# Kernel block 0 of a convolution and feed-forward kernel: bank tiles, buffer order, norm shifts on GpSimd, a split doubling

## The chip, the cores and the metric

The kernel runs on one core of one Trainium2 chip. The metric is the device time of one execution in microseconds. Before the change the median of 3 runs is 1348.77 us (1348.36 to 1349.15).

## The reference

One sequence of 2048 tokens with 576 channels goes through two residual branches, each behind a layer norm whose scale and shift come from a conditioning vector: a long convolution per channel, and a feed-forward layer with 4608 hidden units.

```python
mod = (_silu(c) @ w_mod).reshape(c.shape[0], 6, 1, -1)
sa, ca, ga, sb, cb, gb = (mod[:, 0], ..., mod[:, 5])
h = _layernorm(x) * (1 + ca) + sa
x = x + ga * conv(h)
h = _layernorm(x) * (1 + cb) + sb
x = x + gb * (relu(h @ w1) @ w2)

# conv(u), for L = 2048 and 128 states per channel
dt = exp(log_dt); A = -exp(log_A_real) + 1j * A_imag
C = (C_real + 1j * C_imag) * dt[:, None]
K = 2 * einsum("dn,dnl->dl", C, exp((A * dt[:, None])[:, :, None] * arange(L))).real
y = irfft(rfft(u, 2 * L) * rfft(K, 2 * L), 2 * L)[:, :L] + u * D_skip
```

## The kernel before

The 2048 tokens are four blocks of 512. The feed-forward layer of each block is a long series of matmuls (L1326 and L1351) that starts after the convolution of block 0 and then keeps TensorE occupied to the end. The convolutions of blocks 1 to 3 run as Python generators beside it: `step` in `ffn` takes pieces of them between matmuls, four times for every two series of 14 matmuls, and a piece that yields -1 ends that step. Block 0's convolution, and the kernel K for it, have nothing to hide behind; they fill the first 215 us or so.

The convolution kernel K comes from class `KGen`. The 576 channels are 6 groups of 96 (two halves of 48, index u). An exponent l in the range 0 to 511 is written as 16 times 32, so that K's values for a group are a product of two factor tables: W1 (16 powers, times C) and W2 (32 powers). `first` does this for the groups in three chunks of two groups:

- `raw(c)` makes the phases of a chunk (`turns`: ACT scales `th` and rounds it to an integer `k`, DVE subtracts at L133, 22 times) and the magnitudes (`exps`, on ACT). In chunk 1 it also normalizes the input `h` of block 0: `center` on ACT, for all four slices of `h`, and `affine` on GpSimd, for slices 0 and 1.
- `values(g)` turns them into W2, in two calls of `half_values` (odd, then even): sines on ACT into PSUM tiles `s`, cosines on ACT into SBUF tiles `c` (three buffers), products on DVE (L172, L173) and on GpSimd (the helper `pool` at L59, tiles `W<-c,E`). `start` (L179, L201) writes the first entry of W1, `powers` the factors `Zp` and `zs`. A function `then` is called between the two halves.
- `double(g)` fills W1 by doubling in four steps (`doubling`: DVE at L246, L247, L249, L250, for groups 4 and 5 through the helper at L510; the adds of the last step on GpSimd, tiles `W<-T,T`).
- `multiply(g)` multiplies W1 and W2 on TensorE (L262, 384 small matmuls for a group, "product g" in what follows) into one half of the PSUM tile `kps`, and `rows(g)` copies that out on ACT (tile `ke`). For every three groups the result is stored (`kd`, on SP's queue) and loaded again in another layout (`kt`, L1259).

For g in (0, 2) the order of the calls is: raw(g/2 + 1); double, (at g = 0: affine of slices 2 and 3), multiply, for groups g and g + 1; values(g + 2); values(g + 3) with rows(g) between its halves; rows(g + 1). After that come, from `conv0`: the transform of the input (L758, tile `ZU`), double(4), multiply(4) with the transform of K (`ZK`) in between, double(5), multiply(5). ZU takes SBUF space of the factor tiles, the tables of the transform (`early`, two DMAs from `fcu` and `fck` on SP's queue) one of the three buffers of W1.

What orders the work: each engine runs its instructions in a fixed order that the framework's scheduler has settled when the program is built, by the order of the calls and by when it expects inputs to be there. Instructions marked `keep_in_program_order` (on ACT and GpSimd nearly all of these; from `conv0` on also those through `kept`) keep the order of the calls. Waits go by tile: an instruction that reads or writes a tile waits for the earlier instructions on that tile that it conflicts with, and a new tile in a rotating buffer waits until every user of the old one is done.

In blocks 1 to 3, `inverse` does the transform back in four steps (two matmuls at L1019 into one PSUM buffer, then an add on DVE into `x2`), and `conv` runs it for p = 0 beside `spec_K(1)`.

Of the kernel before, what the change touches and what calls it, by code (L numbers as in the profile page):

```python
# [18 lines left out]
P = 128  # L19
# [6 lines left out]
G = 96  # L26
# [20 lines left out]
class KGen:  # L47
# [13 lines left out]
    def open(self, early, late):  # L61
# [6 lines left out]
        self.ph = pool(late, "kg_ph", "right", space=PSUM)  # L68
        self.kps, self.banks = self.ph.tile([P, 2, 512], F32, name="kps"), 0
        self.factors = ExitStack()  # L70
# [4 lines left out]
    def bank(self):  # L75
        self.banks += 1
        return self.kps[:, self.banks % 2]

# [37 lines left out]
    def turns(self, w):  # L116
# [3 lines left out]
        th = self.th[:, w].rearrange(pair, u=2)  # L120
        if w.start:
            t = self.kps[:, :, 384 : 384 + G]
            self.act(t, th, AF.Copy)
            th = t
        for slots in TURNS:
# [22 lines left out]
    def half_values(self, g, W2, E, f, odd):  # L148
# [31 lines left out]
        for u in range(2):  # L180
            uc = slice(u * H, u * H + H)
            p(W2[u][:, 0, hi], c[:, :, uc], Eh[:, :, uc], op=ALU.mult)
            p(W2[u][:, 0, lo][:, ::-1], c[:, 0:n, uc], El[:, 0:n, uc][:, ::-1], op=ALU.mult)
            if not odd:
                nc.gpsimd.tensor_copy(W2[u][:, 0, 23], El[:, 7, uc])
                nc.gpsimd.memset(W2[u][:, 1, 23], 0.0)

    def start(self, g, s15, c15):

        v = self.nc.vector.tensor_tensor  # L190
        W1 = self.W1[g] = self.pc.tile([P, 2, 16, 2, H], F32, tag="W1", bufs=3, name=f"W1_{g}")
        gs = slice(g * G, (g + 1) * G)
# [31 lines left out]

    def doubling(self, g):

        v, p = self.k.v if g > NG - 3 else self.nc.vector.tensor_tensor, self.pool
        W1, Z = self.W1[g], self.Z[g][0]
        flat = "p u a r c -> p u (a r) c"
        for i, m in enumerate((1, 2, 4, 8)):  # L230
            X, out = W1[:, :, 0:m].rearrange(flat), W1[:, :, m : 2 * m]
# [39 lines left out]
    def first(self, setup, mod, norm):  # L271
# [5 lines left out]
        def raw(c):  # L277
# [4 lines left out]
            if c == 1:  # L282
                for i in range(4):
                    center(i)
                for i in range(2):
                    affine(i)
# [29 lines left out]

        def double(g):
            self.doubling(g)
            for u in range(2):
# [18 lines left out]

        load, stats, scale, center, affine = norm
        next(mod)  # L340
# [8 lines left out]
        for g in (0, 2):  # L349
            raw(g // 2 + 1)  # L350
            for i in (g, g + 1):
                double(i)
                if g == 0:
                    affine(i + 2)
                multiply(i)
            values(g + 2, lambda: None)
            if g == 2:
                t = k.early = self.pc.tile([P, 2, 4, 2, P], F32, tag="W1", bufs=3, name="early")
                for i, n in enumerate(("fcu", "fck")):
                    nc.sync.dma_start(out=t[:, i], in_=k.I[n])  # L360
            values(g + 3, lambda: rows(g))
            rows(g + 1)
        yield
        double(4)
        between = yield
# [122 lines left out]
class Body:  # L488
# [164 lines left out]
    def norm0(self, kg):  # L653
# [15 lines left out]

        def center(i):  # L670
            kg.act(h[:, i], h[:, i], AF.Identity, scale=rs[i][:, 3:4], bias=rs[i][:, 4:5])

        def affine(i):
            kg.pool(h[:, i], h[:, i], self.m["ca"], op=ALU.mult)
            kg.pool(h[:, i], h[:, i], self.m["sa"], op=ALU.add)
# [3 lines left out]

        return load, stats, scale, center, affine  # L680

# [188 lines left out]
    def conv(self, s):  # L870
# [76 lines left out]
        def inverse(p, V):  # L947
            ops = lambda n2: [(self.gc[:, n2, c, :], V[:, n2, c]) for c in range(2)]
            return self.inverse(x2, p, ops)

# [60 lines left out]

    def inverse(self, x2, p, ops, order=(0, 2, 1, 3)):

        xv = x2.rearrange("m n (dd p q) -> m n dd p q", dd=4, p=2)
        for n2 in order:
# [8 lines left out]
            self.v(xv[:, n2, :, p], pv, xv[:, n2, :, p], op=ALU.add)  # L1024
            yield 0.45

    def norm2(self, s, x2, xp, st=None):
# [554 lines left out]
```

## Time and profile before

| | us |
|---|---|
| median of 3 runs | 1348.77 |
| the profiled execution | 1344.2 |
| its span, first to last instruction | 1342.4 |
| TensorE busy in the span | 1220.4 (91%) |
| DVE busy | 870.2 (65%) |
| ACT busy | 503.6 (38%) |
| GpSimd busy | 195.1 (15%) |
| mean granted TensorE clock | 0.946 |

Times in the profile count from the span's first instruction. PE is TensorE, PEld its weight loads, DVE is VectorE, ACT is ScalarE, POOL is GpSimd, SP the engine whose queue issues most DMAs. "L133" is line 133 of the kernel. A row of the timeline has start, length, engine, line, operation, output and inputs, shapes and a count; the brackets give idle time before it and what ended it. Neighbouring instructions of one kind are merged into one row, and instructions of one engine overlap a little, so that the length of one is somewhat more than the distance to the next.

### The profile page before, as it was taken

What the parts mean: (1) busy time and instruction counts of PE and PEld (TensorE: products, weight loads), DVE (VectorE), ACT (ScalarE), POOL (GpSimd) and SP (SyncE); (2) the same over time, 40 slices, a digit from 0 to 9 for tenths busy, and PEclk for the clock granted to TensorE, in tenths of its full rate; (3) what the DMA queues carried; (4) which work ended last, traced back from release to release, by engine and by line L of the source; (5) the groups of instructions that cost most, each with busy time, mean ns of one, the idle gap of its engine ahead of it and who ended that gap; (6) DMA issues with size and microseconds to landing.
All of it is one profiled execution on the core that took longest, in us unless ns stands there. A gap on an engine that the chain in (4) does not pass through costs nothing.

```text
span 1342.4 us, 26042 instructions
## 1 busy us (share of the span) xinstructions
PE 1220.4 (91%) x10608; PEld 974.6 (73%) x10608; DVE 870.2 (65%) x1351; ACT 503.6 (38%) x1014; POOL 195.1 (15%) x271
## 2 busy tenths in 40 slices
PE   5124798999999998999999899999999999999998
PEld 3124566788787786787777787787888888888886
DVE  5978997999887899389546886276988222111111
ACT  7986234222224322622243225343322353232331
POOL 1777231111120100111101000100010000000000
PEclk9555898899999998999999999999999999999999
DMA  6676399888798875698779894757997556666651
GB/s 198 239 256 230 133 365 373 330 290 299 272 362 284 307 277 183 215 396 324 242 262 320 284 356 149 260 183 278 318 347 232 170 181 212 197 197 201 194 169 62
DMA packets 132424, 340.47 MB, mean 254 GB/s; under 512 B 22352, under 2 KB 22672, under 8 KB 132304
## 3 DMA queue, kind: packets, MB, share of 16 engines
q1 hardware_dynamic: 105200, 215.21, 48.3%
q0 software_dynamic: 26816, 123.01, 25.0%
q8 instruction: 83, 1.36, 0.4%
q10 hardware_dynamic: 288, 0.59, 0.1%
q14 instruction: 37, 0.30, 0.1%
HBM read 258.55 MB, written 80.22 MB: 252 GB/s over the span
## 4 chain that ended last, share of the span: by engine, by line
PE 74%; DVE 10%; DMA 7%; issue 5%; ACT 2%; POOL 1%; SPq 0%; DVEq 0%; ACTq 0%; POOLq 0%
PE hps L1326 30%; PE acc L1351 29%; PE kps L440 5%; PE ps_f L758 3%; PE kps L262 3%; DMA Ua<-Ud 3%; DVE T L510 2%; PE ps_i L1019 2%; DMA Ud<-U 1%; DVE k L133 1%; DVE Y L510 1%; DMA W1d<-W 1%; PE kps L607 1%; ACT c L56 1%; DVE W L510 1%
## 5 line engine op out<-in xcount | busy, mean ns | idle before, releaser
L1351 PE MATMUL acc<-hh,w 128*128 128x512 f32 x1296 | 420.5, 400 | 2.1 <-DVE w L510 2.0
L1326 PE MATMUL hps<-xh,w 128*128 128x512 f32 x1152 | 396.2, 404 | 1.9 <-ACT xh L1082 1.9
L1351 PEld LDWEIGHTS acc<-hh,w 128*128 128x128 f32 x1296 | 243.9, 189 | 55.1 <-DVE w L510 2.8
L1332 DVE SCALAR_TENSOR_TENSOR hl<-hps,hh 128x512 fp32r<-128x512 f32 x144 | 99.2, 689 | 279.1 <-ACT hh L1331 278.9
L1351 PE MATMUL acc<-hl,w 128*128 128x512 f32 x720 | 279.9, 399 | 0.0
L1326 PEld LDWEIGHTS hps<-xh,w 128*128 128x128 f32 x1152 | 218.2, 190 | 50.1 <-ACT xh L1082 3.5
L1326 PE MATMUL hps<-xl,w 128*128 128x512 f32 x576 | 231.3, 402 | 0.2 <-DVE xl L1087 0.2
L1331 ACT ACTIVATE hh<-hps 128x512 fp32r<-128x512 f32 x144 | 86.1, 598 | 341.7 <-PE hps L1326 329.5
L1304 ACT ACTIVATE w<-r 128x576 fp32r<-128x576 f32 x144 | 98.7, 686 | 237.5 <-issue 182.8
L1351 PEld LDWEIGHTS acc<-hl,w 128*128 128x128 f32 x720 | 135.8, 189 | 28.1
L1326 PEld LDWEIGHTS hps<-xl,w 128*128 128x128 f32 x576 | 109.5, 190 | 24.9 <-DVE xl L1087 1.5
L262 PE MATMUL kps<-W,W 128*32 128x16 f32 x2304 | 40.3, 217 | 73.4 <-POOL W L59 49.5
L1297 ACT ACTIVATE w<-r 128x640 fp32r<-128x640 f32 x142 | 104.0, 732 | 3.0 <-DMA r<-in_w_dram 3.0
L1326 PE MATMUL hps<-xs,w 128*128 128x512 f32 x288 | 97.4, 418 | 3.5 <-DVE hl L1332 3.4
L262 PEld LDWEIGHTS kps<-W,W 128*32 128x32 f32 x2304 | 37.9, 150 | 77.6 <-POOL W L59 50.9
L510 DVE TENSOR_TENSOR Y<-Y,T 128x1152 f32<-128x1152 f32 x64 | 84.9, 1353 | 0.1
L440 PEld LDWEIGHTS kps<-W1r,W2r 128*32 128x32 f32 x3456 | 63.7, 146 | 23.2 <-issue 17.7
L440 PE MATMUL kps<-W1r,W2r 128*32 128x48 f32 (+2 forms) x3456 | 71.1, 237 | 4.4 <-issue 4.3
L759 ACT ACTIVATE Z<-ps_f 128x288 f32<-128x288 f32 x104 | 42.3, 407 | 64.9 <-PE ps_f L758 62.5
L1326 PEld LDWEIGHTS hps<-xs,w 128*128 128x128 f32 x288 | 53.2, 190 | 16.5 <-DVE hl L1332 4.8
L510 DVE TENSOR_TENSOR W<-Z 128x576 f32<-128x576 f32 x52 | 37.0, 755 | 39.9 <-ACT Z L759 39.7
L510 DVE TENSOR_TENSOR w<-r,w 128x512 fp32r<-128x512 f32 (+2 forms) x108 | 58.2, 578 | 2.9 <-ACT w L1304 2.9
(216 smaller groups left out, 1366.7 us busy)
## 6 DMA issues: line engine op xcount, KB each, us to landing
r<-in_w_dram SPq DMA_DIRECT2D x144, 320.0 KB, 4.0
r<-in_w_dram SPq DMA_DIRECT2D x144, 288.0 KB, 3.6
w<-L1d SPq DMA_DIRECT2D x108, 320.0 KB, 3.0
w<-L2d SPq DMA_DIRECT2D x108, 288.0 KB, 3.1
W2r<-W2d POOLq DMA_DIRECT2D x18, 1536.0 KB, 9.2
W2d<-W SPq DMA_DIRECT2D x10, 1536.0 KB, 7.4
W<-W1d POOLq DMA_DIRECT2D x18, 768.0 KB, 9.2
Ua<-Ud POOLq DMA_DIRECT2D x12, 1152.0 KB, 9.9
```

What stands on the lines that cost most here:

```text
L262: self.nc.tensor.matmul(ps[32 * dd : 32 * dd + 32, 12 * u + q, :], W2[:, r, :, ch], W1[:, u, :, r, ch], start=(r == 0), stop=(r == 1),)
L440: nc.tensor.matmul(ps[32 * dd : 32 * dd + 32, q, :], W2[:, r, :, ch], W1[:, :na, r, ch], start=(r == 1), stop=(r == 0),)
L510: return self.kept(self.nc.vector.tensor_tensor(*args, **kw))
L758: kept(nc.tensor.matmul(o, fc[:, n2, c, :], src(n2), start=True, stop=True))
L759: nc.scalar.activation(Z[:, n2, c], ps[:, :PC], AF.Copy)
L1019: self.nc.tensor.matmul(ps[:, :PC], a, b, start=(i == 0), stop=(i == len(todo) - 1))
L1297: nc.scalar.activation(w[:, 0], r, AF.Copy)
L1304: nc.scalar.activation(w[:, 0:D], r2[g], AF.Copy)
L1326: nc.tensor.matmul(ps, a, x, start=(i == 0), stop=(i == 13))
L1331: nc.scalar.activation(hh, ps, AF.Relu)
L1332: nc.vector.scalar_tensor_tensor(hl, ps, 0.0, hh, op0=ALU.max, op1=ALU.subtract)
L1351: nc.tensor.matmul(acc[i], a, x, start=(f == 0 and j in (0, 3, 6, 9, 12)), stop=(f == NF - 1 and j in (2, 5, 8, 11, 13)),)
```

## The change

- The PSUM tile `kps` with two banks becomes two tiles of one bank each. The copy of `th` into that tile, made for chunks 1 and 2, is dropped with it: L133 then reads `th` from SBUF.
- `center` goes. `affine(i)` subtracts the mean and multiplies by the reciprocal root in one tensor_scalar on GpSimd ahead of its two other instructions. For slices 0 and 1 it stays in raw(1); for slices 2 and 3 it moves from between the doublings to the end of the round g = 0, behind rows(1).
- Doubling takes a list of steps. Steps 0 and 1 of groups 2 and 4 run inside values(g + 3), behind rows(g); steps 2 and 3 where the whole doubling was.
- `place(5)` allocates W1 of group 5 ahead of the tables.
- The copy at L185 is kept in program order.
- In blocks 2 and 3, for p = 0, `inverse` yields -1 after each of its four adds.

```diff
--- before.py
+++ after.py
@@ -66,7 +66,7 @@
         self.pa, self.ss = pool(early, "kg_a", "left"), pool(early, "kg_s", "left", space=PSUM)
         self.pw, self.pc = (pool(late, f"kg_{x}", "right") for x in "wc")
         self.ph = pool(late, "kg_ph", "right", space=PSUM)
-        self.kps, self.banks = self.ph.tile([P, 2, 512], F32, name="kps"), 0
+        self.kps, self.banks = [self.ph.tile([P, 512], F32, name=f"kps{i}") for i in range(2)], 0
         self.factors = ExitStack()
         self.pt = pool(self.factors, "kg_t", "right")
         self.ps = pool(self.factors, "kg_ps", "right", space=PSUM)
@@ -74,7 +74,7 @@
 
     def bank(self):
         self.banks += 1
-        return self.kps[:, self.banks % 2]
+        return self.kps[self.banks % 2]
 
     def setup(self, I):
         nc, pc = self.nc, self.pc
@@ -118,10 +118,6 @@
         F = []
         pair = "p (u c) -> p u c"
         th = self.th[:, w].rearrange(pair, u=2)
-        if w.start:
-            t = self.kps[:, :, 384 : 384 + G]
-            self.act(t, th, AF.Copy)
-            th = t
         for slots in TURNS:
             n = len(slots)
             k = self.pa.tile(
@@ -182,13 +178,18 @@
             p(W2[u][:, 0, hi], c[:, :, uc], Eh[:, :, uc], op=ALU.mult)
             p(W2[u][:, 0, lo][:, ::-1], c[:, 0:n, uc], El[:, 0:n, uc][:, ::-1], op=ALU.mult)
             if not odd:
-                nc.gpsimd.tensor_copy(W2[u][:, 0, 23], El[:, 7, uc])
+                self.tc.keep_in_program_order(nc.gpsimd.tensor_copy(W2[u][:, 0, 23], El[:, 7, uc]))
                 nc.gpsimd.memset(W2[u][:, 1, 23], 0.0)
 
+    def place(self, g):
+        if g not in self.W1:
+            self.W1[g] = self.pc.tile([P, 2, 16, 2, H], F32, tag="W1", bufs=3, name=f"W1_{g}")
+        return self.W1[g]
+
     def start(self, g, s15, c15):
 
         v = self.nc.vector.tensor_tensor
-        W1 = self.W1[g] = self.pc.tile([P, 2, 16, 2, H], F32, tag="W1", bufs=3, name=f"W1_{g}")
+        W1 = self.place(g)
         gs = slice(g * G, (g + 1) * G)
         T = self.ps.tile([P, 512], F32, tag="T", name="Tc")[:, : 2 * G]
         T = T.rearrange("p (x u c) -> p x u c", x=2, u=2)
@@ -222,12 +223,13 @@
             p(zs[:, :, r], zs[:, :, r], e[:, 4:6], op=ALU.mult)
         self.Z[g] = Z, zs
 
-    def doubling(self, g):
+    def doubling(self, g, steps):
 
         v, p = self.k.v if g > NG - 3 else self.nc.vector.tensor_tensor, self.pool
         W1, Z = self.W1[g], self.Z[g][0]
         flat = "p u a r c -> p u (a r) c"
-        for i, m in enumerate((1, 2, 4, 8)):
+        for i in steps:
+            m = 1 << i
             X, out = W1[:, :, 0:m].rearrange(flat), W1[:, :, m : 2 * m]
             zr, zi = (
                 Z[:, r, i].rearrange("p (u c) -> p u c", u=2).unsqueeze(2).broadcast_to([P, 2, 2 * m, H])
@@ -280,8 +282,6 @@
                 scale()
             F = self.turns(w)
             if c == 1:
-                for i in range(4):
-                    center(i)
                 for i in range(2):
                     affine(i)
             E = dict((m, self.exps(w, m)) for m in (2, 3, 0, 1, 4))
@@ -314,8 +314,10 @@
             for u in range(2):
                 save(k.Zd[2 * g + u], zs[:, :, :, u * H : u * H + H], g == NG - 1)
 
-        def double(g):
-            self.doubling(g)
+        def double(g, steps=range(4)):
+            self.doubling(g, steps)
+            if steps[-1] < 3:
+                return
             for u in range(2):
                 save(
                     strips(k.W1d[2 * g + u], 2),
@@ -336,7 +338,7 @@
             if g % 3 == 2:
                 self.store(0, g // 3, ke[0].rearrange("p a q -> p (a q)"), nc.sync)
 
-        load, stats, scale, center, affine = norm
+        load, stats, scale, affine = norm
         next(mod)
         load()
         raw(0)
@@ -349,19 +351,21 @@
         for g in (0, 2):
             raw(g // 2 + 1)
             for i in (g, g + 1):
-                double(i)
-                if g == 0:
-                    affine(i + 2)
+                double(i, range(2, 4) if i == 2 else range(4))
                 multiply(i)
             values(g + 2, lambda: None)
             if g == 2:
+                self.place(5)
                 t = k.early = self.pc.tile([P, 2, 4, 2, P], F32, tag="W1", bufs=3, name="early")
                 for i, n in enumerate(("fcu", "fck")):
                     nc.sync.dma_start(out=t[:, i], in_=k.I[n])
-            values(g + 3, lambda: rows(g))
+            values(g + 3, lambda: (rows(g), double(g + 2, range(2))))
             rows(g + 1)
+            if g == 0:
+                for i in (2, 3):
+                    affine(i)
         yield
-        double(4)
+        double(4, range(2, 4))
         between = yield
         multiply(4, between)
         yield
@@ -667,17 +671,17 @@
         def scale():
             rs.extend(self.norms(st, True))
 
-        def center(i):
-            kg.act(h[:, i], h[:, i], AF.Identity, scale=rs[i][:, 3:4], bias=rs[i][:, 4:5])
-
         def affine(i):
+            self.tc.keep_in_program_order(self.nc.gpsimd.tensor_scalar(
+                h[:, i], h[:, i], rs[i][:, 0:1], rs[i][:, 3:4], op0=ALU.subtract, op1=ALU.mult
+            ))
             kg.pool(h[:, i], h[:, i], self.m["ca"], op=ALU.mult)
             kg.pool(h[:, i], h[:, i], self.m["sa"], op=ALU.add)
 
         def load():
             self.nc.sync.dma_start(out=h, in_=self.I["x"][0].rearrange("n m d -> m n d"))
 
-        return load, stats, scale, center, affine
+        return load, stats, scale, affine
 
     def pool(self, ctx, name, **kw):
         return ctx.enter_context(
@@ -946,7 +950,7 @@
 
         def inverse(p, V):
             ops = lambda n2: [(self.gc[:, n2, c, :], V[:, n2, c]) for c in range(2)]
-            return self.inverse(x2, p, ops)
+            return self.inverse(x2, p, ops, spaced=s > 1 and p == 0)
 
         def back(p, Y):
             V = self.spec(f"V_{s}_{p}")
@@ -1009,7 +1013,7 @@
             v(y, y, T, op=op or ALU.add)
             yield 1.35
 
-    def inverse(self, x2, p, ops, order=(0, 2, 1, 3)):
+    def inverse(self, x2, p, ops, order=(0, 2, 1, 3), spaced=False):
 
         xv = x2.rearrange("m n (dd p q) -> m n dd p q", dd=4, p=2)
         for n2 in order:
@@ -1023,6 +1027,8 @@
             pv = ps[:, :PC].rearrange("m (dd q) -> m dd q", dd=4)
             self.v(xv[:, n2, :, p], pv, xv[:, n2, :, p], op=ALU.add)
             yield 0.45
+            if spaced:
+                yield -1
 
     def norm2(self, s, x2, xp, st=None):
 
```

## The prediction

> **What bounds the kernel now.** I read the clock first, then busy time by stretches, then the chain of waits and the list of who waits for whom over the first 200 us.
>
> ```profile
> 76.00:90.00 14.00, 4.19 (x248) 3.87 (x241) 7.63 (x20) 9.61 (x22) 14.00 (x21) 0.50 0.56 211
> 90.00:104.00 14.00, 0.00 (x0) 0.00 (x0) 13.83 (x41) 13.97 (x52) 4.68 (x8) 0.50 0.78 271
> 118.00:132.00 14.00, 6.50 (x254) 4.92 (x246) 7.77 (x20) 9.70 (x20) 14.00 (x22) 0.50 0.85 303
> 300.00:1342.00 1042.00, 1025.52 (x6911) 822.95 (x6909) 613.12 (x851) 346.45 (x619) 77.20 (x110) 0.99 0.74 250
> ```
>
> Columns: stretch, length, busy time of PE, weight load, DVE, ACT, GpSimd, granted clock, DMA share, GB/s. From 300 us on TensorE is busy 1025.5 of 1042 us: what is won ahead of it shifts everything behind it. Ahead of it the bound changes hands: GpSimd is busy 14.0 of 14.0 in 76 to 90 and in 118 to 132 (half_values), DVE and ACT in 90 to 104 (turns, exps, doubling), while TensorE waits.
>
> ```profile
> 81.85 1.70 PE kps L262 x88
> 83.58 0.49 ACT ke L56
> 84.06 0.73 ACT c L56
> 89.66 5.91 DVE k L133 x22
> ```
> ```profile
> ACT ke L56 <- PE kps L262: 18.6, 3, 13.5
> DVE W L179 <- PE kps L262: 2.7, 1, 2.7
> ACT c L56 <- POOL W L59: 2.5, 1, 2.5
> 79.72 3.75 POOL L59 TENSOR_TENSOR W<-c,E 128x384 f32<-128x384 f32 x4
> ```
>
> The chain goes from product 1 into ACT's copy `ke` of product 0 at 83.58: a wait by tile, since product 0 is the first half of those matmuls. Then come group 3's even half, and the turns of groups 4 and 5 (L133) at 89.66.
>
> **The change part by part.**
>
> *Two bank tiles.* The `ke` copies of rows(0) and rows(2) stop waiting for the next product. Alone this is worth almost nothing: ACT's next `c` needs a buffer that GpSimd reads until 79.72 + 3.75 = 83.47, the same moment as 83.58. What makes it pay is that GpSimd gets there earlier.
>
> *Norm on GpSimd.*
>
> ```profile
> 51.97 3.13 ACT L56 ACTIVATE h<-h,mv 128x576 f32<-128x576 f32 x4
> L59 POOL TENSOR_TENSOR h<-h,m_sa 128x576 f32<-128x576 f32 x4 | 5.7, 1435 | 0.2
> L59 POOL TENSOR_TENSOR h<-h,m_ca 128x576 f32<-128x576 f32 x4 | 5.7, 1414 | 4.5 <-ACT h L56 4.5
> L59 POOL TENSOR_TENSOR zs<-zs,E 128x192 f32<-128x192 f32 x12 | 6.9, 604 | 0.0
> L185 POOL COPY W<-E 128x48 f32<-128x48 f32 x12 | 2.7, 228 | 30.5 <-ACT E L56 30.5
> ```
>
> ACT loses four instructions, 3.13 us, ahead of exps; DVE is still doubling when exps end, so I cost that at nothing. The tensor_scalar (one tensor input, 576 columns) isn't in the trace: not under the 0.60 of an op a third as wide, not over the 1.43 of two inputs; I take 0.8, nearer the low end, since a one-input COPY of 48 columns costs 0.23 in all. affine for two slices is then 2 x (0.8 + 1.41 + 1.44) = 7.3 us. affine(0) and (1) start 4.5 us sooner than now. affine(3), 2.85 us, leaves the stretch that GpSimd bounds: `c` no longer waits 2.5, and the turns at 89.66 come about 2.8 earlier. But affine(2) and (3) now stand behind half_values(3) in GpSimd's queue, ahead of the adds of double(2), and those feed TensorE.
>
> *The PSUM copy of th goes.* The title doesn't say so, but L133 now reads `th` and `k` both from SBUF, while GpSimd has work. The one place that shows such a meeting:
>
> ```profile
> 174.84 2.75 DVE L510 TENSOR_TENSOR W<-Z 128x576 f32<-128x576 f32 x4
> 177.63 3.37 DVE L510 TENSOR_TENSOR U<-W 128x576 f32<-128x576 f32 x6
> 176.15 2.10 POOL L1130 TENSOR_TENSOR kt<-kt,fcU 1x288 f32<-1x288 f32 x1 [11.04 <-DMA kt<-kd]
> 155.53 2.90 DVE L510 TENSOR_TENSOR U<-W 128x576 f32<-128x576 f32 x6
> ```
>
> By the widths above the GpSimd op should take 0.8; it took 2.10, ending at 178.25, just past the end of the four back-to-back DVE ops (177.59). DVE lost about 0.5 afterwards (3.37 for six ops that take 2.90 undisturbed at 155.53). So a running stream of DVE ops with two SBUF inputs shuts GpSimd out, and one GpSimd op in flight delays DVE once. L133 is such a stream, 22 ops in 5.91. In turns of chunk 1 the 4.5 us idle above covers most of it. In chunk 2 nothing does: GpSimd loses 5.9, DVE about 0.5 (bounds: 0 and 5.9 for GpSimd).
>
> *Split doubling.* Steps 0 and 1 of group 2 move ahead of the turns, into DVE's waits for ACT:
>
> ```profile
> 95.48 0.35 DVE L247 TENSOR_TENSOR T<-W,Zp 128x192 f32<-128x192 f32 x1
> 96.32 0.55 DVE L246 TENSOR_TENSOR t<-W,Zp 128x384 f32<-128x384 f32 x1
> 98.04 0.55 DVE L246 TENSOR_TENSOR t<-W,Zp 128x384 f32<-128x384 f32 x1
> 68.71 3.94 POOL L59 TENSOR_TENSOR W<-T,T 128x384 f32<-128x384 f32 x4 [0.99 <-DVE T L247]
> 92.27 1.17 POOL L59 TENSOR_TENSOR zs<-zs,E 128x192 f32<-128x192 f32 x2
> 102.98 3.93 POOL L59 TENSOR_TENSOR W<-T,T 128x384 f32<-128x384 f32 x4 [0.34 <-DVE T L247]
> ```
>
> From 95.48 to 98.04, 2.6 us leave the path; the same again for group 4. DVE would be ready for the adds of 102.98 at 102.98 - 2.8 - 2.6 + 0.5, about 98. GpSimd isn't: now it works without a real pause from 68.71 to 93.44, that is 24.7 us; less 2.85, plus 7.3, plus 5.9 makes 35.1, so the adds start at about 104, not 98. **GpSimd takes DVE's place**, and product 2 starts 1 us later than now. Double(3) and the halves behind it still gain: their GpSimd work runs on without a pause, about 4 us earlier than now.
>
> *Group 5's tile ahead of the tables.* W1_5 takes the buffer that product 2 frees, so DVE's 2.7 us wait goes. The tables take the one that product 3 frees.
>
> ```profile
> 104.03 0.30 PE L262 MATMUL kps<-W,W 128*32 128x16 f32 x2 [20.50 <-POOL W L59]
> 124.22 1.72 PE L262 MATMUL kps<-W,W 128*32 128x16 f32 x99 [1.56 <-issue]
> 116.78 0.37 SPq L360 DMA_DIRECT2D early<-in_fcu_dram  x1
> early<-in_fcu_dram SPq DMA_DIRECT2D x1, 512.0 KB, 6.2
> 133.11 0.71 ACT L759 ACTIVATE ZU<-ps_f 128x288 f32<-128x288 f32 x2 [2.16 <-POOL W L59]
> 140.77 0.28 PE L262 MATMUL kps<-W,W 128*32 128x16 f32 x2 [2.05 <-POOL W L59]
> 166.27 6.55 PE L758 MATMUL ps_f<-h,early 128*128 128x288 f32 x16
> ```
>
> Products 2 and 3 take 104.03 to 125.94, 21.9 us, with waits between instruction blocks rather than on data. One later start: 127; table issued, 6.2 to landing: 133.2; the 16 matmuls of ZU, 6.55: product 4 at 139.8, 1.0 ahead of 140.77. The stores of `kd` stand behind the tables on SP's queue, and DVE waits for the reload of `kt` between doubling 4 and 5, so DVE's large lead (2.6 + 4 + 2.7) also shrinks, to about 3. I take 2 for the whole stage, between 1 and 3; the DMA-bound stretch after it starts that much earlier with the same work.
>
> *A yield after each inverse step of blocks 2 and 3.*
>
> ```profile
> 764.26 0.40 PE L1351 MATMUL acc<-hl,w 128*128 128x512 f32 x1
> 768.72 2.29 PE L1019 MATMUL ps_i<-V,gc 128*128 128x288 f32 x4 [4.06 <-DVE x L510]
> 790.00:800.00 10.00, 10.00 (x46) 8.27 (x45) 10.00 (x9) 3.14 (x5) 0.00 (x0) 1.00 1.04 391
> 800.00:810.00 10.00, 10.00 (x46) 8.29 (x45) 10.00 (x10) 2.60 (x4) 0.00 (x0) 1.00 0.72 219
> ```
>
> TensorE idles 4.06 us before block 2's second inverse step, for DVE. The yield puts that step one stop later, seven matmuls of 10.00 / 46 = 0.22 us, 1.6 us of other work in the gap. I take 1.6 won. Bounds: the whole 4.06 and, below nothing, 3 lost: three stops with little in them, and DVE already full at 790 to 810 ahead of block 2's end.
>
> Sum: -2 - 1.6 = -3.6 against the profiled execution, 1344.2 us (span 1342.4): 1340.6. The runs' median, 1348.77, lies 4.6 above it: **1345.2**.
>
> **The rivals.**
>
> 1. *GpSimd is not shut out.* Drop the 5.9: adds at 98, product 3 done at 121, table there by 127; GpSimd's last `c` reads, which hold up ZU now until 133.11, end about 6 earlier; kt comes early too. Stage gain 6, with the yield 7.6: 1341. For it: one meeting in the trace is thin evidence, and L133 ops, 0.27 apart, wait for ACT one by one and may leave gaps.
>
> 2. *GpSimd and DVE take turns op by op* (slower). Each L133 then waits for one GpSimd op while GpSimd has any queued. In chunk 1 nine are queued: the last `c` product, two zs and six of affine, some 1.0 + 1.2 + 7.3 = 9.5 us, so L133 ends about 9 later, and again in chunk 2; the gains above (2.8, twice 2.6, 2.7) give back some 10 of 18: +8, 1356. It decides when more than about four GpSimd ops get in per chunk. Against it: the op at 176.15 let DVE's later, independent ops pass. [...]
>
> 3. *The queue behind GpSimd and the yields cost more.* With tensor_scalar at 1.43, four times 0.63 more, product 3 ends 2.5 later, so product 4 starts 1.5 later than now, and the yields lose 3: +4.5, 1353.
>
> That the copies wait for the bank and not the tile, so that splitting does nothing, is excluded by `ke` at 83.58.
>
> **How the numbers follow.** Forecast 0.49, its own range 1342.5 to 1348.5; rival 1 0.27; rival 2 0.12; rival 3 0.12. A measurement here can tell about 0.2%, 2.7 us, from no change. Faster: rival 1 and six tenths of the forecast, 0.56. Same: the rest of the forecast and half of rival 3, 0.26. Slower: 0.18. The range 1339.5 to 1351.5 takes in the bounds of the port and of the yields and leaves out rival 2 and the far ends of 1 and 3.
>
> **What would show it.** In the changed profile: `ke` of rows(0) well before product 1 ends; the turns of chunk 2 starting near 86.5; GpSimd with a hole of some 6 us during them and the adds of double(2) near 104; the table's issue just after product 3, near 127; product 4 near 140; the idle before the second inverse step of block 2 at 2.5 us. I am wrong if GpSimd runs through the turns (rival 1), if L133 spreads over far more than 6 us (rival 2), or if product 4 starts after 141 (rival 3).

## The result, and the profile after

The changed kernel takes 1358.18 us (median of 6 runs, 1354.83 to 1359.42) against 1348.57 for the kernel before on the same chip (6 runs, 1343.22 to 1349.15). The ratio is 1.0071, with a 95% interval of 1.0052 to 1.0089: **slower by 0.7%**, where 1345.2 was forecast and 1351.5 was the upper end of the range. The profiled execution of the changed kernel took 1354.83 us (span 1353.0).

First the groups of instructions by line of the kernel before, from 40 to 125 us (busy time in us and mean of one in ns behind the first bar):

```profile
L133 DVE SCALAR_TENSOR_TENSOR k<-kps,k 128x192 f32<-128x192 f32 x44 | 11.9, 351 | 0.0
```

The same view and stretch of the kernel after:

```profile
L129 DVE SCALAR_TENSOR_TENSOR k<-th,k 128x192 f32<-128x192 f32 x44 | 26.2, 667 | 0.0
...
L675 POOL TENSOR_SCALAR h<-h,mv 128x576 f32<-128x576 f32 x4 | 10.7, 2673 | 0.0
L59 POOL TENSOR_TENSOR h<-h,m_ca 128x576 f32<-128x576 f32 x4 | 6.0, 1494 | 0.3
```

The 44 turns of chunks 1 and 2 grew from 11.9 to 26.2 us. The new tensor_scalar takes 2.67 us, not 0.8 and not under 1.43. Next the busy time by stretches of the kernel after (length, then PE, weight load, DVE, ACT, GpSimd, clock, DMA share, GB/s):

```profile
48.00:62.00 14.00, 0.00 (x0) 0.00 (x0) 14.00 (x25) 13.97 (x52) 13.26 (x11) 0.50 0.66 240
96.00:109.00 13.00, 0.00 (x0) 0.00 (x0) 13.00 (x25) 12.97 (x48) 12.84 (x12) 0.50 0.84 294
300.00:1353.00 1053.00, 1034.61 (x6955) 829.73 (x6954) 624.43 (x862) 349.51 (x624) 77.90 (x112) 0.99 0.74 251
```

The first two rows are the turns of chunks 1 and 2: DVE counts as busy throughout, and GpSimd too. There is no 6 us hole in GpSimd's work, as there would be if DVE shut it out. From 300 us on TensorE is as full as before. The loss lies ahead of it: the first matmul of block 0's FFN comes 12.5 us later. Of these, 10.6 reach the end of the span (1353.0 against 1342.4).

```profile
212.44 0.71 PE L1326 MATMUL hps<-xs,w 128*128 128x512 f32 x2
```

```profile
224.94 0.73 PE L1332 MATMUL hps<-xs,w 128*128 128x512 f32 x2 [0.29 <-DVE xs L1091]
```

(The first fence is the timeline of the kernel before, the second that of the kernel after: start, duration, engine, line, operation; in brackets the idle time before and what ended it.)

**How a turn waits.** The timeline of GpSimd, and then of DVE, in chunk 1 of the kernel after, single instructions:

```profile
52.75 1.52 POOL L59 TENSOR_TENSOR h<-h,m_ca 128x576 f32<-128x576 f32 x1
54.35 1.40 POOL L59 TENSOR_TENSOR h<-h,m_sa 128x576 f32<-128x576 f32 x1
55.73 2.76 POOL L675 TENSOR_SCALAR h<-h,mv 128x576 f32<-128x576 f32 x1
...
52.94 1.54 DVE L129 SCALAR_TENSOR_TENSOR k<-th,k 128x192 f32<-128x192 f32 x1
...
54.41 1.56 DVE L129 SCALAR_TENSOR_TENSOR k<-th,k 128x192 f32<-128x192 f32 x1
...
55.88 0.34 DVE L129 SCALAR_TENSOR_TENSOR k<-th,k 128x192 f32<-128x192 f32 x1
```

The turn at 52.94 ends at 54.48, 0.21 after the product of GpSimd that began at 52.75 (it ends at 54.27). The next turn, at 54.41, ends at 55.97, 0.22 after the sum of 54.35. Here one turn goes through per GpSimd instruction. Beside the tensor_scalar at 55.73, with a single tensor as input, a turn takes 0.34 again: of the eight turns that begin during its 2.76 us seven take 0.34 or 0.35, one 0.81. The c products of chunk 2 show the same pairs, GpSimd first in each:

```profile
96.29 1.00 POOL L59 TENSOR_TENSOR W<-c,E 128x336 f32<-128x336 f32 x1
96.46 1.04 DVE L129 SCALAR_TENSOR_TENSOR k<-th,k 128x192 f32<-128x192 f32 x1
...
97.55 1.11 POOL L59 TENSOR_TENSOR W<-c,E 128x384 f32<-128x384 f32 x1
97.72 1.15 DVE L129 SCALAR_TENSOR_TENSOR k<-th,k 128x192 f32<-128x192 f32 x1
```

That is rival 2 of the prediction: turns of 13.8 us in chunk 1 (48.0 to 61.8) and 12.4 us in chunk 2 (96.2 to 108.6). Its 1356 lies within the changed kernel's runs.

**Product 3.** A second loss was in no rival. TensorE's timeline of the kernel after, from the end of product 2 on, and SP's queue beside it:

```profile
127.05 2.11 PE L264 MATMUL kps<-W,W 128*32 128x16 f32 x128 [1.53 <-issue]
132.97 2.15 PE L264 MATMUL kps<-W,W 128*32 128x16 f32 x128 [3.81 <-issue]
139.72 1.80 PE L264 MATMUL kps<-W,W 128*32 128x16 f32 x99 [4.60 <-issue]
...
153.56 0.28 PE L264 MATMUL kps<-W,W 128*32 128x16 f32 x2 [1.15 <-POOL W L59]
...
127.24 0.37 SPq L361 DMA_DIRECT2D early<-in_fcu_dram  x1
132.73 2.40 SPq L296 DMA_DIRECT2D W2d<-W  x2
```

Product 3 runs from 124.8 to 141.5; from its first matmul's start to its last one's it takes 16.5 us instead of 11.3. There are two gaps of 3.81 and 4.60 us between groups of 128 matmuls, ended by nothing but "issue". The kernel before has 2.17 and 1.56 there:

```profile
120.51 2.15 PE L262 MATMUL kps<-W,W 128*32 128x16 f32 x127 [2.17 <-issue]
```

The second long gap, up to 139.72, lies beside group 4's two W2d stores. The first, up to 132.97, is over 0.24 us after the first of these is issued; it lies beside the table load of 127.24 and the last W1d store before it. The W2d stores, as the list of DMA issues of the kernel after has them (KB each, us from issue to landing):

```profile
W2d<-W SPq DMA_DIRECT2D x2, 1536.0 KB, 8.1
```

Product 4 starts at 153.56 instead of 140.77. The first write of group 5's tile still waits for product 3:

```profile
141.61 0.42 DVE L175 TENSOR_TENSOR W<-tc,Tc 128x96 f32<-128x96 f32 x2 [6.27 <-PE kps L264]
```

So "group 5's tile ahead of the tables" did not take effect: the tables were issued at 127.24, behind product 2 and its last store, and group 5's tile waited for product 3, as in the kernel before.

### The profile page after: what moved, and what is told of

It reads as the page before. It is cut to its first block, busy times and chain, and to the rows that moved or that the text cites. A ratio compares the mean times of both kernels' runs of the same rounds, so it can differ in the third digit from the quotient of the medians.

```text
span 1353.0 us, 26036 instructions
## 1 busy us (share of the span) xinstructions
PE 1217.9 (90%) x10608; PEld 970.6 (72%) x10608; DVE 883.8 (65%) x1351; ACT 500.0 (37%) x1008; POOL 206.6 (15%) x275
## 4 chain that ended last, share of the span: by engine, by line
PE 68%; DVE 14%; DMA 9%; issue 5%; ACT 2%; POOL 2%; SPq 0%; DVEq 0%; ACTq 0%; POOLq 0%
PE hps L1332 28%; PE acc L1357 27%; PE kps L444 5%; PE ps_f L762 3%; DVE T L514 3%; DMA Ua<-Ud 3%; DVE Y L514 2%; DVE k L129 2%; PE kps L264 2%; DMA Ud<-U 1%; PE kps L611 1%; PE ps_i L1023 1%; DMA W1d<-W 1%; DMA Ka<-Rd 1%; DMA r<-in_w_dram 1%
## 5 line engine op out<-in xcount | busy, mean ns | idle before, releaser
L1303 ACT ACTIVATE w<-r 128x640 fp32r<-128x640 f32 x142 | 104.0, 732 | 10.9 <-DMA r<-in_w_dram 10.9
L1332 PEld LDWEIGHTS hps<-xs,w 128*128 128x128 f32 x288 | 53.1, 191 | 16.6 <-DVE hl L1338 4.4
## 6 DMA issues: line engine op xcount, KB each, us to landing
W2r<-W2d POOLq DMA_DIRECT2D x18, 1536.0 KB, 10.2
Ua<-Ud POOLq DMA_DIRECT2D x12, 1152.0 KB, 10.2
```

The lines of the kernel that those rows point to most:

```text
L1303: nc.scalar.activation(w[:, 0], r, AF.Copy)
L1332: nc.tensor.matmul(ps, a, x, start=(i == 0), stop=(i == 13))
```

## The experiments

Theory A: in the turns a DVE instruction with two SBUF inputs and GpSimd's instructions exclude each other, one by one, and that is what costs. Theory B: the slow tensor_scalar, or GpSimd's longer queue, makes the turns long, wherever `th` lies. Theory C: the tensor_scalar alone. Theory F came with the results: product 3 is stretched by traffic.

One table for all, each row from the run's trace and its times; us, where "turns" is the time from the first to the last of 22, "adds" the first GpSimd add of double(2), P2 to P4 the products (P3 from its first matmul's start to its last one's), FFN the first matmul of block 0's FFN. The ratio is to the kernel before on the same chip. From FFN to the end of the span these twelve profiles take between 1123.0 us (e8) and 1134.0 (e6), so a microsecond in that column need not be one in the time.

| kernel | turns 1 | turns 2 | adds | P2 starts | P3 takes | P4 starts | FFN | ratio (95%) |
|---|---|---|---|---|---|---|---|---|
| before | 6.0 | 5.9 | 103.0 | 104.0 | 11.3 | 140.8 | 212.4 | 1 |
| after | 13.8 | 12.4 | 113.4 | 114.5 | 16.5 | 153.6 | 224.9 | 1.0071 (1.0052 to 1.0089) |
| e1_th_psum | 5.9 | 5.9 | 103.9 | 105.0 | 16.1 | 144.0 | 216.8 | 1.0032 (1.0014 to 1.0050) |
| e2_before_th_sbuf | 7.6 | 9.9 | 110.4 | 111.4 | 17.1 | 154.2 | 225.4 | 1.0046 (1.0027 to 1.0066) |
| e3_center_act | 7.9 | 16.3 | 113.0 | 114.0 | 16.4 | 153.3 | 224.7 | 1.0063 (1.0037 to 1.0089) |
| e5_psum_center | 5.9 | 5.9 | 99.3 | 100.4 | 16.6 | 140.2 | 211.3 | 0.9979 (0.9961 to 0.9996) |
| e6_hold_stores4 | 5.9 | 5.9 | 100.0 | 101.0 | 12.6 | 135.8 | 218.3 | 1.0049 (1.0029 to 1.0069) |
| e7_no_yields | 5.9 | 5.9 | 99.9 | 100.9 | 16.4 | 140.2 | 211.2 | 0.9965 (0.9944 to 0.9986) |
| e8_tables_behind5 | 5.9 | 5.9 | 101.8 | 102.9 | 15.4 | 142.0 | 221.0 | 1.0005 (0.9982 to 1.0028) |
| e9_unsplit | 5.9 | 5.9 | 101.7 | 102.7 | 11.8 | 138.0 | 210.8 | 0.9980 (0.9953 to 1.0008) |
| e10_stores_after_kt | 5.9 | 5.9 | 101.0 | 102.0 | 14.3 | 139.5 | 211.1 | 0.9953 (0.9937 to 0.9969) |
| e11_after_stores | 12.5 | 14.0 | 112.7 | 113.8 | 12.6 | 149.4 | 221.3 | 1.0055 (1.0032 to 1.0078) |

### e1_th_psum: the PSUM copy put back into the changed kernel

```diff
         th = self.th[:, w].rearrange(pair, u=2)
+        if w.start:
+            t = self.ps.tile([P, 512], F32, tag="T", name="th_t")[:, : 2 * G].rearrange(pair, u=2)
+            self.act(t, th, AF.Copy)
+            th = t
```

> The changed kernel with one thing put back: in chunks 1 and 2 the turns (L129) read th from a copy in PSUM (in the 192 columns of the bank that the doubling uses for T) instead of from SBUF. Theory A (a DVE op with two SBUF inputs and a GpSimd op wait for one another op by op, so the port is what costs): the turns of chunk 1 and of chunk 2 take 5.9 us each again instead of 13.8 and 12.4, product 0 starts near 61.5 instead of 69.4, chunk 2's turns near 88, the first adds of double(2) near 104, block 0's FFN near 213 to 216 instead of 224.9; time 1345 to 1350, about 10 under the changed kernel. Theory B (the turns are long because of the slow tensor_scalar or because of GpSimd's queue, whatever th lies in): the turns still take over 9 us each and the time stays above 1354. In passing: the tensor_scalar on GpSimd beside turns that have one SBUF input; 0.8 to 1.4 us if its 2.4 to 2.8 were waiting for the port, still 2.4 or more if that is its price.

Both stretches of turns are back to 5.9 us, and the median falls from 1358.18 to 1349.95. (FFN, expected at 213 to 216, comes at 216.8.) DVE's timeline, and behind it GpSimd's in the same stretch:

```profile
47.45 5.90 DVE L133 SCALAR_TENSOR_TENSOR k<-th_t,k 128x192 f32<-128x192 f32 x22
...
49.45 2.29 POOL L679 TENSOR_SCALAR h<-h,mv 128x576 f32<-128x576 f32 x1
51.82 1.41 POOL L59 TENSOR_TENSOR h<-h,m_ca 128x576 f32<-128x576 f32 x1
```

The 22 turns run straight through beside GpSimd's instructions, and those have the 1.41 of the kernel before. Theory A holds, B falls. The second half of the question is settled too: the four tensor_scalars take 2.29 us on average beside turns with one SBUF input, so 0.4 of the 2.67 came with `th` in SBUF and the rest is their price.

### e2_before_th_sbuf: the kernel before without the PSUM copy

```diff
-        if w.start:
-            t = self.kps[:, :, 384 : 384 + G]
-            self.act(t, th, AF.Copy)
-            th = t
```

> The kernel before with only the PSUM copy of th taken out, so that its turns (L129 here) read two SBUF tiles; GpSimd has no affine to do during chunk 1's turns, and in chunk 2's it has the last c products and two zs, until 93.4. Theory A: chunk 1's turns stay at 6 us; chunk 2's, which start at 89.7, grow by the 3.7 us of GpSimd work that is queued then, to about 9.5; time +1 to +4 against before. Theory B: both stay at 6 us and the time is that of before within 1.

Chunk 2's turns take 9.9 us where 9.5 was expected of A, chunk 1's 7.6 instead of 6. This one removal makes the old kernel slower by 0.46%, some 6 us, more than the 1 to 4 expected. DVE's and GpSimd's timelines:

```profile
92.79 4.27 DVE L129 SCALAR_TENSOR_TENSOR k<-th,k 128x192 f32<-128x192 f32 x1
...
91.11 4.64 POOL L59 TENSOR_TENSOR W<-c,E 128x384 f32<-128x384 f32 x5
95.70 1.14 POOL L59 TENSOR_TENSOR zs<-zs,E 128x192 f32<-128x192 f32 x2
```

Here GpSimd's c products and zs, which end at 96.84, went one behind the other, and the first turn, from 92.79, had to wait for all of them, 4.27 us for that one. So the turns need not alternate; the time lost, 4.0 us, is that of the GpSimd work from 92.79 to 96.84, 4.05. Behind the turns product 3 is stretched here too, to 17.1 us.

### e3_center_act: the shift back on ACT, th in SBUF

```diff
         def affine(i):
-            self.tc.keep_in_program_order(self.nc.gpsimd.tensor_scalar(
-                h[:, i], h[:, i], rs[i][:, 0:1], rs[i][:, 3:4], op0=ALU.subtract, op1=ALU.mult
-            ))
...
+        def center(i):
+            kg.act(h[:, i], h[:, i], AF.Identity, scale=rs[i][:, 3:4], bias=rs[i][:, 4:5])
...
             if c == 1:
+                for i in range(4):
+                    center(i)
```

> The changed kernel with the norm's shift back on ACT (four Identity activations of 3.1 us in all ahead of chunk 1's exps, no tensor_scalar on GpSimd); th stays in SBUF. Theory A: in chunk 1 affine now waits for ACT until the turns are nearly over, so GpSimd has little to do and the turns take about 6 us; in chunk 2 the c products, zs and the products and sums of affine(2) and (3), without the tensor_scalar, are queued, and the turns still take 9 to 12. Time 1346 to 1352. Theory C (the tensor_scalar alone is the cause): both chunks' turns go back to 6 us and the time to 1344 to 1347.

Theory C falls: the time stays within the uncertainty of the changed kernel's. At 1356.22 it misses the 1346 to 1352 that A expected, too. Chunk 1 gets better (7.9, where A expected about 6), but chunk 2 takes 16.3 us, more than A's 9 to 12: its turns begin 4.4 us earlier than in the changed kernel and meet more of GpSimd's list. The groups of GpSimd's instructions from 92 to 107 us:

```profile
L59 POOL TENSOR_TENSOR W<-c,E 128x384 f32<-128x384 f32 (+1 forms) x6 | 6.2, 1059 | 0.0
L59 POOL TENSOR_TENSOR h<-h,m_ca 128x576 f32<-128x576 f32 x2 | 3.0, 1516 | 0.0
L59 POOL TENSOR_TENSOR h<-h,m_sa 128x576 f32<-128x576 f32 x2 | 2.8, 1400 | 0.2
L59 POOL TENSOR_TENSOR zs<-zs,E 128x192 f32<-128x192 f32 x2 | 1.4, 702 | 0.0
```

That is twelve instructions with two inputs and 13.4 us. Less 12 x 0.27, the pace at which the turns would have run anyway (5.9 / 22), 10.2 are left, nearly all of 16.3 - 5.9 = 10.4. In chunk 1 GpSimd met the opposite fate (GpSimd first, then DVE):

```profile
55.58 3.17 POOL L59 TENSOR_TENSOR h<-h,m_ca 128x576 f32<-128x576 f32 x1 [3.69 <-ACT h L56]
...
53.91 3.57 DVE L129 SCALAR_TENSOR_TENSOR k<-th,k 128x192 f32<-128x192 f32 x13
```

This GpSimd instruction came out of a wait of 3.69 us into a running stream of turns, and took 3.17 instead of 1.41: it ended 1.3 after the stream's last turn (57.48), so it was shut out until then. That is the behaviour the prediction took for the rule.

### e5_psum_center: both together

The edits of e1 and e3 in one kernel.

> The changed kernel with th in PSUM for chunks 1 and 2 and the shift on ACT: what is left of the change is the two bank tiles, the split doubling, group 5's tile, affine(2) and (3) moved behind, and the yields. Theory A: turns of 5.9 us in both chunks; GpSimd's queue is 5 us shorter in chunk 2 than with tensor_scalars, so the adds of double(2) start near 99 to 101 (before: 103.0) and the time comes out under before, 1341 to 1346. If moving affine(2) and (3) behind half_values(3) is what costs, then the adds come at 103 or later and the time is 1347 or more.

The adds come at 99.3 as expected (99 to 101), and the median is 1345.17 against 1348.03, faster than before by 0.2%, as A expected. From e1 to e5 the ratio falls from 1.0032 to 0.9979 and FFN from 216.8 to 211.3: that is the price of four tensor_scalars on GpSimd, once the turns are out of the way. But double(2)'s adds come 3.7 us earlier than before, and product 4 only 0.6. TensorE's timeline:

```profile
119.96 2.16 PE L268 MATMUL kps<-W,W 128*32 128x16 f32 x128 [4.05 <-issue]
126.43 1.73 PE L268 MATMUL kps<-W,W 128*32 128x16 f32 x99 [4.31 <-issue]
```

Product 3 again: 16.6 us. The runs e6 and e9 to e11 bear on why.

### e6_hold_stores4: group 4's W2d stores out of product 3

```diff
-                    W2[u].rearrange("p r (y b) c -> p (r y) (b c)", y=2), g == NG - 1,
+                    W2[u].rearrange("p r (y b) c -> p (r y) (b c)", y=2), g >= NG - 2,
...
-            for dst, src in self.held[:2]:
+            for dst, src in self.held[:4]:
...
-            for dst, src in self.held[2:]:
+            for dst, src in self.held[4:]:
```

> The kernel of e5_psum_center with group 4's two W2d stores (768 KB each, in e5 issued at 118.5 and 120.5, in the middle of product 3) held back and sent with group 5's, after the reload of kt. Theory F (product 3 is stretched because its instruction blocks are fetched beside full DMA queues: gaps of 4.1 and 4.3 us, marked issue, in e5 where the kernel before has 1.2 to 2.2): product 3 takes 12 to 14 us instead of 16.6, group 5's first write on DVE stops waiting 5.9 us for it, product 4 starts 2 to 4 us sooner than 140.2; time 1341 to 1345, if the DMA-bound stretch after 180 doesn't take the 1.5 MB back (then 1344 to 1347). Rival: the gaps belong to the program and not to the traffic: product 3 stays over 16 and product 4 at 140.

Product 3 does what theory F said, and the total is wrong. It takes 12.6 us, and product 4 starts 4.4 earlier than in e5. (On SP's queue the second table load moves up with it, from 124.2 to 114.3.) But the expectation had the stores at half their size: they are 1536 KB each, and 3 MB more in the stretch that DMA bounds (DMA share 1.03 in the kernel before from 180 to 212 us, 1.01 to 1.05 in e5 from 180 to 215) cost far more than was won:

```profile
121.88 1.78 PE L268 MATMUL kps<-W,W 128*32 128x16 f32 x99 [2.40 <-issue]
...
210.33 3.86 PE L643 MATMUL mps_gb<-wm_gb,cb 128*32 128x128 f32 x50 [11.20 <-DMA wm_gb<-in_w_mod_dram]
```

TensorE waits 11.20 us for a weight load that now stands behind those stores, 23.9 from issue to landing; FFN comes 7 later than in e5, the time 0.7% higher.

### e7_no_yields

```diff
-            return self.inverse(x2, p, ops, spaced=s > 1 and p == 0)
+            return self.inverse(x2, p, ops, spaced=False)
```

> The kernel of e5_psum_center without the yields after the inverse steps of blocks 2 and 3. Block 0 as in e5 (double(2)'s adds at 99.3). If the yields win what the prediction said: TensorE's idle before block 2's second inverse step goes from 2.6 back to about 4, and the time up by 1 to 1.6. Rival: they only move the idle (0.8 before block 2's fourth step and 0.5 in block 3 go away again), and the time is that of e5 within 1.

TensorE's timeline of e5, then of this kernel:

```profile
769.87 1.65 PE L1029 MATMUL ps_i<-V,gc 128*128 128x288 f32 x4 [2.63 <-DVE x L520]
...
815.25 1.21 PE L1029 MATMUL ps_i<-V,gc 128*128 128x288 f32 x4 [0.81 <-DVE V L520]
```

```profile
764.98 2.29 PE L1029 MATMUL ps_i<-V,gc 128*128 128x288 f32 x4 [3.59 <-DVE x L520]
```

With the yields the idle before block 2's second inverse step is 2.63 us (4.06 in the kernel before), and an idle of 0.81 appears later in the same block, 3.44 in all; without them the first is 3.59 and the second is gone. In the changed kernel the two are 1.74 and 2.25. The time without the yields is 0.14% lower than e5's, with intervals that overlap. The yields move the idle; a gain from them is not to be seen.

### e8_tables_behind5: group 5's tile really first

```diff
-            if g == 2:
-                self.place(5)
-                t = k.early = self.pc.tile([P, 2, 4, 2, P], F32, tag="W1", bufs=3, name="early")
-                for i, n in enumerate(("fcu", "fck")):
-                    nc.sync.dma_start(out=t[:, i], in_=k.I[n])
             values(g + 3, lambda: (rows(g), double(g + 2, range(2))))
+            if g == 2:
+                t = k.early = self.pc.tile([P, 2, 4, 2, P], F32, tag="W1", bufs=3, name="early")
+                for i, n in enumerate(("fcu", "fck")):
+                    nc.sync.dma_start(out=t[:, i], in_=k.I[n])
```

> The kernel of e5_psum_center with the two table loads issued behind group 5's values, so that group 5's tile really takes the buffer that product 2 frees and the tables the one that product 3 frees (in the changed kernel, as in the one before, group 5's first write still waits for product 3). DVE's wait of 5.9 us ahead of group 5's first write goes and double(4) is ready earlier; the tables are issued at product 3's end, about 127 instead of 113, and land some 6 us later, so the 16 matmuls that read them start near 134 instead of 129.9. Theory T (the tables decide): product 4 starts at 142 to 144 instead of 140.2, time +1 to +4 against e5. The prediction's step: product 4 starts about 1 sooner, time -1 to -2.

DVE's wait for product 3 is gone. TensorE now waits for the tables:

```profile
134.92 7.14 PE L767 MATMUL ps_f<-h,early 128*128 128x288 f32 x16 [6.07 <-DVE T L519]
```

(The table loads were issued at 128.9 and 129.8; the releaser named in the row is a DVE instruction long done.) Product 4 starts at 142.0, 1.8 later than in e5, as theory T said, and not 1 sooner. The median is 3.9 higher, with intervals that overlap: the order that the change's title speaks of wins nothing here, and that it costs time is not shown.

### e9_unsplit: doubling in one piece

```diff
-                double(i, range(2, 4) if i == 2 else range(4))
+                double(i)
...
-            values(g + 3, lambda: (rows(g), double(g + 2, range(2))))
+            values(g + 3, lambda: rows(g))
...
-        double(4, range(2, 4))
+        double(4)
```

> The kernel of e5_psum_center with the doublings of groups 2 and 4 in one piece again, behind the turns. Theory: their first two steps, 2.6 us of DVE, come back behind the turns, the adds of double(2) come at 101.5 to 102 instead of 99.3 and product 2 as much later; of that, product 3's stretch decides how much reaches product 4: time +0 to +2.5 against e5. Rival: GpSimd and not DVE decides when the adds start, as the prediction held: the adds stay at 99 to 100 and the time that of e5.

GpSimd's timeline of e5, then of e9:

```profile
99.33 1.97 POOL L59 TENSOR_TENSOR W<-T,T 128x384 f32<-128x384 f32 x2
```

```profile
101.69 1.97 POOL L59 TENSOR_TENSOR W<-T,T 128x384 f32<-128x384 f32 x2 [2.52 <-DVE T L253]
```

The split is worth 2.4 us on these adds, as the prediction's 2.6 said, and afterwards GpSimd has no pause left (no bracket in the first row). Yet product 4 starts 2.2 us *earlier* without the split, and the two times can't be told apart. In e5 the stores are issued 7.2 us after product 3's start (118.5 against 111.3), in e9 8.5 us after it (121.1 against 112.6), and product 3 takes 11.8 us instead of 16.6: its last two gaps are 1.86 and 1.58. What the split wins, product 3 gives back.

### e10_stores_after_kt and e11_after_stores: the stores into the idle stretch

In e7's kernel (e10) and in the changed kernel (e11) group 4's two W2d stores go right behind the reload of `kt`:

```diff
         kt = [self.load_kt(0, 0)]
+        with tc.issue_after(self.ktd.ins):
+            for dst, src in self.held[:2]:
+                nc.sync.dma_start(out=dst, in_=src)
```

(with the first edit of e6, and held[2:4] and held[4:] at the two later places).

> The kernel of e7_no_yields (th in PSUM, shift on ACT, no yields) with group 4's two W2d stores issued right behind the reload of kt, at about 129, into the stretch 135 to 150 where e5's DMA share falls to 0.01. Theory F: product 3 takes 12.6 us as in e6_hold_stores4 instead of 16.4, product 4 starts near 136 instead of 140.2 and, unlike in e6, nothing is added to the DMA-bound stretch after 180: block 0's FFN near 207 to 209 instead of 211.2, time 1339 to 1342. Rival: the stores now meet the instruction blocks of product 4, or the DMA-bound stretch takes up any lead: the time stays at 1343 to 1345.

> The changed kernel as it is (th in SBUF, tensor_scalar on GpSimd, yields) with the same move of group 4's two W2d stores. Theory F: product 3 takes about 12.5 us instead of 16.5, product 4 starts near 149 instead of 153.6 and FFN near 221 instead of 224.9: time 3 to 5 under the changed kernel, about 1354. Rival: the lead is taken up in the DMA-bound stretch, and the time stays at 1357 to 1359.

TensorE's timeline of e11:

```profile
129.53 2.15 PE L264 MATMUL kps<-W,W 128*32 128x16 f32 x128 [1.89 <-issue]
134.63 1.77 PE L264 MATMUL kps<-W,W 128*32 128x16 f32 x99 [2.95 <-issue]
```

In e11 product 3 takes 12.6 us, product 4 starts 4.1 and FFN 3.6 earlier than in the changed kernel, as F said; the time is 1356.07, 2.1 lower, with overlapping intervals. In e10 the stores are issued at 132.1 and 133.5, and product 3 takes 14.3. Both tables, 1 MB, are now issued 0.3 us after its start, but in e6 and e11 they load during product 3 as well (issued 3.0 and 2.8 us into it), so why e10 gets less is open. Product 4 comes 0.7 earlier than in e7, not 4, and FFN not at all: F's 1339 to 1342 was missed. At 1343.35 against 1349.46, ratio 0.9953 (0.9937 to 0.9969), e10 beats both kernels, and it can't be told apart from e7.

## Why the prediction was wrong

**The step that failed: "the PSUM copy of th goes".** It took one meeting at 176.15, where DVE's stream ran on and GpSimd waited, for the rule: "a running stream of DVE ops with two SBUF inputs shuts GpSimd out", at 5.9 us for GpSimd and 0.5 for DVE. It was the other way round: DVE lost 7.9 and 6.5 us, GpSimd hardly anything (its products with `m_ca` took 1.49 instead of 1.41, the tensor_scalars 2.67 instead of the 2.29 of e1). The row at 176.15 was read rightly, and e3 shows the same thing at 55.58; but there GpSimd's instruction came out of a wait into a running stream. In the turns GpSimd's instructions stand one behind the other, and in each of these traces a turn then waits for one of them (1.54 us at 52.94) or for several (4.27 us in e2). For chunk 1 the prediction also let the meeting go with "the 4.5 us idle above covers most of it", though its own norm change takes that idle away: GpSimd is busy 13.26 of the 14 us from 48 to 62. What the prediction should have asked is who has work queued, and GpSimd's list was known: the work "without a real pause" that it had just added up to 35.1 us. Rival 2 had mechanism, place and size ("L133 ends about 9 later" in chunk 1: 61.8 against 52.8) and got 0.12 of the chance. That its 1356 came out is partly luck: it charged chunk 2 with 9 (measured: 6.5) and counted 2.7 back for group 5's tile, which brought nothing, but it left out product 3's 5.2.

Which of the two waits doesn't follow from which began first. In the pairs at 52.75 and 96.29 GpSimd began 0.2 us ahead, and the turn ended 0.2 behind it, after 1.54 and 1.04 us instead of 0.34. But six turns that began after 55.58 in e3, and five GpSimd instructions that began after 92.79 in e2, went ahead of the one that was waiting. Nor did every GpSimd instruction hold a turn up: beside the tensor_scalar at 55.73 the turn at 55.88 took 0.34. The port of the recorded texts is the author's guess, which no run shows; the runs show the times alone.

**Mis-sized: the tensor_scalar.** It was taken at 0.8 with an upper bound of 1.43, "not over the 1.43 of two inputs". It takes 2.29 beside turns with one SBUF input (e1), against 1.41 for a product with two inputs of that width, so the bound had no ground; e1 to e5 puts the price of four of them at 5.5 us of the stage. That is rival 3's mechanism, at more than its price.

**Taken as fixed: product 3.** The 21.9 us of products 2 and 3, "with waits between instruction blocks rather than on data", were carried over as a constant. They are 27.0 in the changed kernel (114.5 to 141.5), because TensorE's last two gaps in product 3 are longer there: 3.81 and 4.60 us instead of 2.17 and 1.56. In e6, e9 and e11 product 3 takes 11.8 to 12.6. The stores' own place hardly moved: they came 8.1 us into product 3 in the kernel before, 7.9 in the changed one. What moved is the packet of the instruction queue ahead of the last group of matmuls, which started ahead of them before and starts behind them now (the last section has the times).

**Right, but worth less.** The copy `ke` of product 0 comes ahead of product 1's end (91.3). ACT's timeline of the kernel after:

```profile
88.09 0.47 ACT L56 ACTIVATE ke<-kps 128x384 f32<-128x384 f32 x1
```

"GpSimd takes DVE's place": in e1, where the turns are as the prediction had them, the adds come at 103.9 (forecast 104) straight behind affine, and product 2 at 105.0 (forecast 105). That GpSimd sets the start is right; that the figure fits is luck. The 5.9 us of shut-out in it did not occur, but two tensor_scalars took 4.6 us instead of 1.6, the stretch began at 70.2 instead of 68.7, and GpSimd waited 1.05 us for product 1, 5.6 in all. The start of chunk 2's turns came 0.8 to 1.2 earlier in e1 and e5, not 2.8.

**Wrong without much effect.** Group 5's tile took no other buffer, so the 1.0 us at product 4 had nothing to stand on; the line was read and not the waits that would follow from it, which only the changed trace shows. The yields' 1.6 us (seven matmuls of 0.22 are 1.5) is not found.

The account of the changed kernel's 12.5 us at FFN, from one profile of each kernel: th in SBUF 8.1 (after to e1), the tensor_scalars 5.5 (e1 to e5), the rest -1.1, in which the split and the bank tiles have won and product 3 has lost. The parts don't add freely: with th in SBUF, taking the tensor_scalars away (e3) brings 0.2 us. In the ratios the same three steps are 0.39%, 0.53% and -0.21%, that is 5, 7 and -3 us.

## What to carry over

Before an operand moves from PSUM to SBUF on DVE, add up GpSimd's queued two-input work at that moment: DVE's stretch grew by about all of it here (by 10.4 us beside 10.2 in e3, by 4.0 beside 4.05 in e2), and one row in which GpSimd lost doesn't say who loses next. What is won ahead of a stretch of many small matmuls need not arrive behind it: the 3.7 us at e5's adds left 0.6 at product 4, with product 3 at 16.6 us, and with two stores held back it took 12.6 (e6). Compare its gaps, and the packets of the instruction queue, with when stores and loads are issued. And an edit that names an order (a tile "ahead of" another) has to be found again in the waits of the new trace.

## What was not expected of the hardware

**Packets of the instruction queue beside DMA.** The view of the DMA queues of the kernel after, from 114 to 142 us:

```profile
q1 hardware_dynamic: 2488, 6.82, 66.4%
q8 instruction: 5, 0.08, 1.3%
```

Five packets of 16 KB on an instruction queue, beside 6.82 MB on the other; TensorE stops every 128 matmuls, each with its weight load. In the kernel before product 3's gaps are 1.15 to 2.17 us, in the changed one, e1 and e5 they reach 3.8 to 5.4. In the traces of the kernel before and the changed one products 0 to 3 have 20 gaps of over 1 us that end with "issue", and each ends 1.2 to 1.5 us after the end of such a packet. That TensorE waits for these packets, and that they are the recorded texts' instruction blocks, is the author's inference from that. The packets ahead of the 20 gaps take 0.9 to 1.8 us, and those ahead of the two of over 3 us 1.04 and 0.92: those of the long gaps are not slower, they come later.

What makes them late is shown only in part. Ahead of the last group of product 3 the packet starts at 122.00 in the kernel before, 0.5 ahead of the first W2d store, and at 137.52 in the changed kernel, 4.8 behind it. But the packet that ends the first long gap runs from 130.46 to 131.50, ahead of that store (132.73). So e6 and e11 show that moving the stores shortens product 3 as a whole (12.6 us instead of 16.6 and 16.5); in the first gap it cannot be the stores' own traffic, and the last W1d store and the table load, which were in flight there, have not been tried alone. Traffic alone doesn't decide: in product 2 of the changed kernel, with a W1d store of 768 KB issued from 115.41 on, the gap up to 119.70 is 1.69. When such a packet is asked for is not in the trace. What the gaps cost is: in product 3 of the changed kernel TensorE is busy 6.77 of the 16.70 us from 124.8 to 141.5.

**One engine, three prices.** A GpSimd product of 576 columns took 1.41 us beside turns that read one SBUF tile (e1), 1.52 between turns that read two (after), and 3.17 when it came into a running stream of them (e3); a tensor_scalar of the same width took 2.29 to 2.76 and held DVE up in at most one turn, of 0.81 to 0.97. What decides, at the moment when both engines have work, which of them goes first stays open: in these traces GpSimd's instruction waited when it came out of a wait (3.17 us instead of 1.41 in e3, 2.10 at 176.15 in the kernel before), and went through when it followed another one directly (1.40 to 1.53 in the changed kernel).
